# Fp32 attention and expert kernel on one core: where the tiles of the on-chip buffer begin

## The chip, the cores and the metric

The kernel runs on one core of a Trainium2 chip. The time is device microseconds of one execution on that core, and lower is better. The core has a matrix engine (PE, whose weight loads the profile lists apart as PEld), a vector engine (DVE), a scalar engine (ACT), a general engine (POOL) and a queue engine (SP) that issues most DMAs. All tiles named below lie in the on-chip buffer, 128 partitions deep; a "place" is the byte at which a tile begins within every partition. Results of matmuls go to another memory of eight banks of 2 KB, which the change doesn't touch.

## The reference

```python
# attention: 2 batches, 8 heads, 768 positions, head size 64; 4 sink positions and a window of 128
scores = scale * np.matmul(q, k.transpose(0, 1, 3, 2))
scores = np.where(is_sink | in_window, scores, -1000000000.0)
a = softmax(scores)
x = (a @ v) laid out as (1536, 512)
# eight experts, 512 -> 1024 -> 512, gate P normalised 8 times by rows and by columns
P = np.exp(logits - logits.max())
for e in range(8):
    out += P[:, e:e + 1] * (np.maximum(x @ w1[e], 0.0) @ w2[e])
# one more layer, 512 -> 2048 -> 512
h = out @ w_in
return (np.maximum(h, 0.0) ** 2) @ w_out
```

## The kernel before

**Split numbers.** Every large matrix is kept as two float tiles, a high part (name ending in h) and a low part (ending in l), and each product is three matmuls: high by high, high by low, low by high. They accumulate into one bank of 512 columns.

**Layers.** The two hidden layers are cut into 20 chunks of 512 hidden units (16 for the experts, 4 for the last layer), and the 1536 tokens into three blocks of 512; chunk 0 alone is worked in blocks of 384 tokens, beside the attention. A step "1" (`mm1`, matmuls at line 451) makes 128 hidden units by one block of tokens: 12 matmuls, in which the 128 by 128 weight piece from a `w0` tile is held in the array and 512 columns of `xh` or `xl` stream through it. A step "2" (`mm2`, line 499) makes 128 tokens by 512 outputs: 12 matmuls, in which a 128 by 128 piece of the hidden tile (`hh` or `hl`) is held and the 512 columns of a `w1` tile stream. Four steps "1" and four steps "2" alternate, 48 matmuls each. In the names of the profile `mm<-xh,w_1l` the streamed operand stands first and the held one second; the digit is the parity of the chunk.

```python
nc.tensor.matmul(
    out=ps[:, 0:n], lhsT=w[:, kc, f * 128 : (f + 1) * 128],   # mm1: held
    rhs=x[:, kc, t0 : t0 + n], ...)                            # mm1: streamed
nc.tensor.matmul(
    out=ps, lhsT=x[:, f, s], rhs=w[:, f, :], ...)              # mm2: held, streamed
```

**Around them.** `mm1_evac` (ACT line 463, DVE line 464) turns a finished bank into `hh` and `hl`; `mm2_evac` (DVE line 517) adds a finished bank to `acc`. Weights come by DMA into `wraw` and are split by ACT (line 389) and POOL (line 390). The gate (line 546) streams `xl` and `xh` through the held tile `wgz`; `x2` (line 527) transposes `acc` into `xh` and `xl` for the last layer. The attention (lines 219 to 357) takes the first 190 us or so and has matmuls of steps "1" and "2" of chunk 0 woven in.

**Order.** The order of instructions on each engine is the order in which the code is written (`manual_schedule`), and nothing in it depends on where a tile lies.

**Places.** Tiles get their places in the order in which pools are opened, each pool behind the one before, rounded to 32 bytes. `run` opens `const`, then `big` (`xh`, `xl`, `acc`, 24,576 bytes each), then `gp` (the gate's small tiles: `P`, `l2`, `mx`, `nm`, `nmb`, `rs`, `cs`, 1,344 bytes in all), then the pools of the weights, the hidden tiles and the rest. In the built program this gives:

| tiles | begin at | past a multiple of 2,048 |
|---|---|---|
| `xh`, `xl`, `acc` | 17,056; 41,632; 66,208 | 672 |
| all `w0`, `w1`, `hh`, `hl`, `wraw`, `wgz` tiles | 92,128 and on, in steps of 8,192 (`wgz` 225,248) | 2,016 |
| `pth`, `ptl` of the attention | 197,472 and on, in steps of 6,144 | 864 |

One row of a `w` or `hh` tile (512 floats) is 2,048 bytes, one row of `xh` 6,144, and a block of 512 tokens 2,048: so a streamed row begins 672 bytes past a multiple in every step "1" of 512 columns, and 2,016 past in every step "2". The held pieces of 512 bytes begin at 2,016, 480, 992 or 1,504 past, in both.

Of the kernel before, what the change touches and what calls it, by code (L numbers as in the profile page):

```python
# [9 lines left out]
F32 = mybir.dt.float32  # L10
# [23 lines left out]
NJ = (3, 4)  # L34
QKW = (QW + KW[0], QW + KW[1])
BIG = 1e30


class Kernel:
# [62 lines left out]
    def masks(self):  # L102
# [9 lines left out]
        )  # L112
        big = dict(scalar1=BIG, scalar2=-BIG, op0=ALU.mult, op1=ALU.add)
        nc.vector.tensor_tensor(out=self.m0, in0=band[:, 128:256], in1=sk[:, 0:128], op=ALU.max)
# [539 lines left out]
    def run(self):  # L654
        nc, tc = self.nc, self.tc
        ctx = self.ctx
        self.const = self.pool(ctx, "const")
        big = self.pool(ctx, "big")
        self.gp = self.pool(ctx, "gp")
        PS = bass.MemoryType.PSUM  # L660
        self.ps_mm = self.pool(ctx, "ps_mm", 2, PS)
        self.ps_sc = self.pool(ctx, "ps_sc", 2, PS)
        self.ps_pt = self.pool(ctx, "ps_pt", 2, PS)
        self.ps_xs = self.pool(ctx, "ps_xs", 2, PS)
        self.xh = big.tile([128, KD, NT], F32R, name="xh")
        self.xl = big.tile([128, KD, NT], F32R, name="xl")
        self.acc = big.tile([128, NTILE, DM], F32, name="acc")
        self.P = self.gp.tile([128, NTILE, E], F32, name="P")
        with ExitStack() as all_:
            self.reset()  # L670
            self.wp = [self.pool(all_, "wp0"), None]
            self.hp = [self.pool(all_, "hp0"), None]
            self.wraw = [self.pool(all_, "wraw0")]
            with tc.manual_schedule():
                gen = self.moe_groups(1)
                with ExitStack() as actx:
                    self.att = self.pool(actx, "att")
                    self.attraw = self.pool(actx, "attraw")
                    self.attv = self.pool(actx, "attv")
                    self.att2 = self.pool(actx, "att2", 2)  # L680
                    self.attp = self.pool(actx, "attp", 2)
                    self.att_load_qk(0)
                    self.masks_begin()
                    self.att3 = self.pool(actx, "att3", 3)
                    fill = self.phase_a(gen)
                self.phase_b(all_, 1, fill, gen)
        with tc.If(nc.values_load(self.flag, min_val=0, max_val=1)):
            with ExitStack() as all_:
                self.reset()
                with tc.manual_schedule():  # L690
                    with ExitStack() as actx:
                        self.tmp = self.pool(actx, "gtmp")
                        self.att = self.pool(actx, "gatt")
                        self.att2 = self.pool(actx, "gatt2", 2)
                        self.general_attention()
                    self.wp = [self.pool(all_, "gwp0"), None]
                    self.hp = [self.pool(all_, "ghp0"), None]
                    self.wraw = [self.pool(all_, "gwraw0")]
                    gen = self.moe_groups(0)
                    self.phase_b(all_, 0, None, gen)  # L700
# [346 lines left out]
```

## Time and profile before

| | us |
|---|---|
| median of three runs (1501.34, 1504.84, 1506.44) | 1504.84 |
| the profiled execution | 1502.89 |
| its span, first to last instruction | 1501.0 |
| busy in that span: PE | 1469.7 |
| DVE | 680.4 |
| ACT | 376.3 |
| POOL | 278.8 |

Matmuls are pipelined: one begins before the one ahead of it has drained, so the rows of the profile overlap, and a matmul's duration in a row is longer than the step from its start to the next start. What a matmul costs on a full PE is the step between two starts, or the length of a piece of the chain of waits divided by its matmuls.

### The profile page before, as it was taken

Reading aid. Unit: us, or ns where it says so; the run is one execution under the profiler, and the core shown is the slowest. Engines: PE = TensorE matmul, PEld = TensorE weight load, DVE = VectorE, ACT = ScalarE, POOL = GpSimd, SP = SyncE. Lnnn points to the kernel's source line nnn. Section 1 sums busy time; section 2 is a strip of 40 time slices with the busy share of each in tenths; the row PEclk is TensorE's granted clock in tenths of the full one; section 3 lists DMA queues with packets and bytes.
Section 4 is the critical chain, followed back from the end, with each engine's and each line's share of the span. In section 5 each row is a group of like instructions: output and inputs, shape, how many; then the busy total and the mean of one; then the engine's idle time right before and its main releaser. Section 6 shows DMA issues by size and latency. Waiting matters only on the chain.

```text
span 1501.0 us, 16714 instructions
## 1 busy us (share of the span) xinstructions
PE 1469.7 (98%) x6791; PEld 1201.9 (80%) x6791; DVE 680.4 (45%) x1372; ACT 376.3 (25%) x807; POOL 278.8 (19%) x238
## 2 busy tenths in 40 slices
PE   5899999999999999999999999999999999999998
PEld 4788887888888888888888888888888888888886
DVE  7988836242222222222222222222223789688732
ACT  5767622211111211111121111112111133232211
POOL 4533312111111211111121111111111112011100
PEclk9899999999999999999999999999999999999999
DMA  3323111000101000000100000010000122011001
GB/s 115 110 59 93 43 76 57 28 29 28 37 22 54 28 28 29 28 28 28 57 29 28 29 28 28 28 57 28 28 29 29 56 85 84 28 57 57 29 22 66
DMA packets 15045, 67.76 MB, mean 45 GB/s; under 512 B 2160, under 2 KB 4208, under 8 KB 8816
## 3 DMA queue, kind: packets, MB, share of 16 engines
q1 hardware_dynamic: 14672, 66.61, 13.3%
q8 instruction: 55, 0.90, 0.2%
q14 instruction: 30, 0.25, 0.1%
q10 hardware_dynamic: 288, 0.00, 0.0%
HBM read 63.46 MB, written 3.15 MB: 44 GB/s over the span
## 4 chain that ended last, share of the span: by engine, by line
PE 93%; DVE 5%; ACT 1%; DMA 0%; issue 0%; ACTq 0%; DVEq 0%
PE mm L451 43%; PE mm L499 43%; PE xp L347 3%; PE sc L219 1%; PE ptp L272 1%; DVE p L259 1%; DVE p L232 1%; DMA wn_i<-window 0%; DVE st L249 0%; PE mm L546 0%; DVE ptl L308 0%; DVE hl L464 0%; PE mm L527 0%; DVE rs L582 0%; ACT qkh L174 0%; ACT p L242 0%
## 5 line engine op out<-in xcount | busy, mean ns | idle before, releaser
L463 ACT ACTIVATE hh<-mm 128x512 fp32r<-128x512 f32 (+1 forms) x196 | 115.3, 588 | 810.3 <-PE mm L451 810.3
L464 DVE SCALAR_TENSOR_TENSOR hl<-mm,hh 128x512 fp32r<-128x512 f32 (+1 forms) x196 | 133.3, 680 | 387.4 <-ACT hh L463 387.4
L517 DVE SCALAR_TENSOR_TENSOR acc<-mm,P,acc 128x512 f32<-128x512 f32 x168 | 125.9, 750 | 279.8 <-PE mm L499 279.8
L451 PE MATMUL mm<-xl,w_0h 128*128 128x512 f32 (+1 forms) x496 | 193.3, 390 | 0.0
L451 PE MATMUL mm<-xh,w_0h 128*128 128x512 f32 (+1 forms) x496 | 193.0, 389 | 0.0
L451 PE MATMUL mm<-xh,w_0l 128*128 128x512 f32 (+1 forms) x496 | 191.9, 387 | 0.0
L451 PE MATMUL mm<-xh,w_1l 128*128 128x512 f32 x480 | 189.7, 395 | 0.0
L451 PE MATMUL mm<-xh,w_1h 128*128 128x512 f32 x480 | 189.3, 394 | 0.0
L451 PE MATMUL mm<-xl,w_1h 128*128 128x512 f32 x480 | 189.3, 394 | 0.0
L499 PE MATMUL mm<-w_0h,hh 128*128 128x512 f32 x480 | 188.1, 392 | 0.0
L499 PE MATMUL mm<-w_0l,hh 128*128 128x512 f32 x480 | 188.0, 392 | 0.0
L499 PE MATMUL mm<-w_1h,hl 128*128 128x512 f32 x480 | 187.4, 390 | 0.0
L499 PE MATMUL mm<-w_1h,hh 128*128 128x512 f32 x480 | 187.2, 390 | 0.0
L499 PE MATMUL mm<-w_0h,hl 128*128 128x512 f32 x480 | 187.1, 390 | 0.0
L499 PE MATMUL mm<-w_1l,hh 128*128 128x512 f32 x480 | 187.0, 389 | 0.0
L390 POOL TENSOR_TENSOR w_1l<-wraw,w_1h 128x512 fp32r<-128x512 f32 x64 | 82.1, 1292 | 434.4 <-ACT w_1h L389 434.4
L390 POOL TENSOR_TENSOR w_0l<-wraw,w_0h 128x512 fp32r<-128x512 f32 x64 | 81.9, 1289 | 368.0 <-ACT w_0h L389 368.0
L451 PEld LDWEIGHTS mm<-xl,w_0h 128*128 128x128 f32 x496 | 92.9, 187 | 21.4 <-issue 1.3
L451 PEld LDWEIGHTS mm<-xh,w_0h 128*128 128x128 f32 x496 | 92.9, 187 | 21.2 <-issue 1.1
L451 PEld LDWEIGHTS mm<-xh,w_0l 128*128 128x128 f32 x496 | 92.9, 187 | 19.9
L451 PEld LDWEIGHTS mm<-xh,w_1h 128*128 128x128 f32 x480 | 89.9, 187 | 22.1
L451 PEld LDWEIGHTS mm<-xl,w_1h 128*128 128x128 f32 x480 | 89.9, 187 | 21.7
(143 smaller groups left out, 1918.1 us busy)
## 6 DMA issues: line engine op xcount, KB each, us to landing
wraw<-w SPq DMA_DIRECT2D x32, 1024.0 KB, 4.9
wraw<-win SPq DMA_DIRECT2D x8, 1024.0 KB, 5.2
wraw<-wout SPq DMA_DIRECT2D x8, 1024.0 KB, 5.1
raw<-qkv SPq DMA_DIRECT2D x8, 624.0 KB, 4.0
raw<-qkv SPq DMA_DIRECT2D x8, 464.0 KB, 3.5
out<-acc SPq DMA_DIRECT2D x12, 256.0 KB, 2.0
vraw<-qkv SPq DMA_DIRECT2D x8, 256.0 KB, 2.7
vraw<-qkv SPq DMA_DIRECT2D x8, 192.0 KB, 2.4
```

The source lines that it names most:

```text
L219: nc.tensor.matmul(out=ps[:, 0:wd], lhsT=x[r, l * 128 : (l + 1) * 128], rhs=y[r, QW + off : QW + off + wd], start=(m == 0), stop=(m == 2),)
L232: self.nc.vector.tensor_tensor_reduce(out=p[:, a, 0:wd], in0=self.sc[u][a][:, 0:wd], in1=mask[a], scale=-(D ** -0.5), scalar=3e38, op0=ALU ...
L259: self.nc.vector.tensor_scalar(out=p[:, a, 0:wd], in0=p[:, a, 0:wd], scalar1=st[:, 2 + a : 3 + a], scalar2=None, op0=ALU.mult,)
L272: nc.tensor.transpose(ps[:, a, j * 128 : (j + 1) * 128], p[:, a, tt[a] + j * 128 : tt[a] + (j + 1) * 128], self.ident,)
L347: nc.tensor.matmul(out=o, lhsT=l, rhs=r, start=(k == 0), stop=(k == last), skip_group_check=True)
L390: nc.gpsimd.tensor_tensor(out=lo[:, s], in0=src, in1=hi.bitcast(F32)[:, s], op=ALU.subtract)
L451: nc.tensor.matmul(out=ps[:, 0:n], lhsT=w[:, kc, f * 128 : (f + 1) * 128], rhs=x[:, kc, t0 : t0 + n], start=(k == 0), stop=(k == 3 * KD - 1),)
L463: nc.scalar.activation(out=hh[:, f, 0:n], in_=ps[:, 0:n], func=AF.Relu)
L464: nc.vector.scalar_tensor_tensor(out=hl[:, f, 0:n], in0=ps[:, 0:n], scalar=0.0, in1=h32[:, f, 0:n], op0=ALU.max, op1=ALU.subtract,)
L499: nc.tensor.matmul(out=ps, lhsT=x[:, f, s], rhs=w[:, f, :], start=(k == 0), stop=(k == 3 * KD - 1),)
L517: nc.vector.scalar_tensor_tensor(out=a, in0=ps, scalar=self.P[:, ti, e : e + 1], in1=a, op0=ALU.mult, op1=ALU.add)
```

## The change

The pool `gp` is opened before `big` instead of behind it, and a pool of one tile of 8 floats (32 bytes) is opened between the two, written once by DVE.

```diff
+PAD = 8
...
         self.const = self.pool(ctx, "const")
+        self.gp = self.pool(ctx, "gp")
+        pad = self.pool(ctx, "pad")
         big = self.pool(ctx, "big")
-        self.gp = self.pool(ctx, "gp")
...
+        nc.vector.memset(pad.tile([128, PAD], F32, name="pad"), 0.0)
         self.xh = big.tile([128, KD, NT], F32R, name="xh")
```

In the built program `xh`, `xl` and `acc` then begin at 18,432, 43,008 and 67,584, that is 1,376 bytes further on and 0 past a multiple of 2,048. Everything behind `acc` moves by 32 bytes: all `w0`, `w1`, `hh`, `hl`, `wraw` and `wgz` tiles begin 0 past a multiple; the attention's tiles move by the same 32 bytes (`pth` 896 past). `ident` stays, and `P` moves to 17,056.

No instruction changes its place on any engine, nor any wait; DVE has one more. The first rows of DVE's order before (line, operation, out and in):

```order
L1043 UNCONDITIONAL_BRANCH
L76 MEMSET warm 128x1
L81 CAST acc<-acc 128x256
L82 CAST acc<-acc 128x256
L62 CAST ns_f<-ns_i 128x1
```

The same place in the changed kernel, where line numbers are one or more higher:

```order
L1047 UNCONDITIONAL_BRANCH
L668 MEMSET pad 128x8
L77 MEMSET warm 128x1
L82 CAST acc<-acc 128x256
L83 CAST acc<-acc 128x256
L63 CAST ns_f<-ns_i 128x1
```

One small write stands ahead of the one that the scalar engine's first table load goes with; nothing else has moved.

## Rows read from the trace of the kernel before

**Rows 1.** The page: span, engines' busy time, granted clock by slices, chain shares.
```profile
span 1501.0 us, 16714 instructions
PE 1469.7 (98%) x6791; PEld 1201.9 (80%) x6791; DVE 680.4 (45%) x1372; ACT 376.3 (25%) x807; POOL 278.8 (19%) x238
...
PEclk9899999999999999999999999999999999999999
...
PE 93%; DVE 5%; ACT 1%; DMA 0%; issue 0%; ACTq 0%; DVEq 0%
```

**Rows 2.** Engines' busy time in stretches: PE, PEld, DVE, ACT, POOL, clock, DMA.
```profile
400.00:800.00 400.00, 400.00 (x1739) 325.69 (x1738) 104.58 (x145) 68.00 (x121) 61.34 (x48) 1.00 0.09 32
```

**Rows 3.** The chain that ended last, in time: start us, us, what.
```profile
1.17 7.05 DMA wn_i<-window
...
263.93 11.23 PE mm L451 x48
275.16 10.90 PE mm L499 x48
286.06 11.20 PE mm L451 x48
297.26 10.90 PE mm L499 x48
...
1192.16 11.20 PE mm L451 x48
1203.36 1.75 PE mm L527 x16
...
1462.68 11.20 PE mm L451 x48
1473.88 21.80 PE mm L499 x96
```

**Rows 4.** Groups by shape: line, engine, names, shapes, count | busy us, mean ns.
```profile
L451 PE MATMUL mm<-xh,w_1l 128*128 128x512 f32 x480 | 189.7, 395 | 0.0
...
L499 PE MATMUL mm<-w_1l,hh 128*128 128x512 f32 x480 | 187.0, 389 | 0.0
L451 PE MATMUL mm<-xh,w_0l 128*128 128x512 f32 x432 | 170.4, 394 | 0.0
...
L451 PE MATMUL mm<-xh,w_0l 128*128 128x384 f32 x64 | 21.6, 337 | 0.0
```

**Rows 5.** Timeline of PE at the border of two blocks: start us, us, what.
```profile
804.93 0.39 PE L451 MATMUL mm<-xl,w_1h 128*128 128x512 f32 x1
805.17 0.39 PE L451 MATMUL mm<-xh,w_1h 128*128 128x512 f32 x1
805.40 0.39 PE L499 MATMUL mm<-w_1h,hl 128*128 128x512 f32 x1
...
806.55 0.39 PE L499 MATMUL mm<-w_1l,hh 128*128 128x512 f32 x1
806.78 0.39 PE L499 MATMUL mm<-w_1h,hl 128*128 128x512 f32 x1
```

**Rows 6.** Timeline of PE: 384-column matmuls at two places, and the gate's.
```profile
126.50 0.34 PE L451 MATMUL mm<-xh,w_0h 128*128 128x384 f32 x1
...
127.36 0.34 PE L451 MATMUL mm<-xl,w_0h 128*128 128x384 f32 x1
...
205.44 0.40 PE L546 MATMUL mm<-xh,wgz 128*128 128x512 f32 x1
...
206.84 0.40 PE L546 MATMUL mm<-xh,wgz 128*128 128x512 f32 x1
207.07 0.34 PE L451 MATMUL mm<-xl,w_0h 128*128 128x384 f32 x1
...
208.81 0.34 PE L451 MATMUL mm<-xh,w_0h 128*128 128x384 f32 x1
...
212.08 0.34 PE L451 MATMUL mm<-xh,w_0h 128*128 128x384 f32 x1
...
213.85 0.34 PE L451 MATMUL mm<-xh,w_0l 128*128 128x384 f32 x1
```

**Rows 7.** Groups by shape, weight loads of both lines.
```profile
L451 PEld LDWEIGHTS mm<-xh,w_0l 128*128 128x128 f32 x496 | 92.9, 187 | 19.9
L499 PEld LDWEIGHTS mm<-w_0l,hh 128*128 128x128 f32 x480 | 90.1, 188 | 19.3 <-issue 0.7
```

**Rows 8.** Timeline of all engines at the start.
```profile
0.80 0.06 DVE L76 MEMSET warm<- 128x1 f32 x1 [0.80 <-PEq L1033]
...
1.21 0.40 DVE L81 CAST acc<-acc 128x256 f32<-128x256 int32 x1 [0.34 <-POOL acc L79]
...
1.67 1.28 ACT L77 ACT_TABLE_LOAD   x1 [1.67 <-PEq L1033]
...
2.96 0.20 ACT L77 ACTIVATE warm<-warm 128x1 f32<-128x1 f32 x1
5.73 1.07 ACT L174 ACTIVATE qkh<-raw 128x640 fp32r<-128x640 f32 x2 [2.56 <-DMA raw<-qkv]
```

**Rows 9.** Groups by shape: transposes of the attention and of `x2`, and the gate.
```profile
L272 PE MATMUL ptp<-ident,p 128*128 128x128 f32 x176 | 32.9, 307 | 8.3 <-DVE p L259 8.3
...
L527 PE MATMUL mm<-ident,acc 128*128 128x128 f32 x48 | 5.7, 273 | 0.0
...
L546 PE MATMUL mm<-xl,wgz 128*128 128x512 f32 x12 | 4.9, 412 | 0.0
```

## The prediction

> **What bounds the kernel now.** I read the page first. PE is busy for 1469.7 of 1501.0 us, the chain that ended last is 93% PE, and the granted clock is full in nearly every slice [rows 1]. DVE, ACT and POOL have 45% and less, so an operation of theirs counts only where PE waits for it. From 264 us to the end PE never waits: the chain of waits is one row of blocks of 48 matmuls [rows 3], and a stretch of 400 us in the middle has 400.00 us of PE at clock 1.00, the 2.4 GHz level [rows 2]. What can move the time is therefore the step from one matmul's start to the next, not a wait.
>
> The chain gives that step for the two kinds of block. A block of line 451 takes 11.20 us, 233.3 ns a matmul; a block of line 499 takes 10.90 us, 227.1 ns [rows 3]. Both stream 512 columns, hold 128 by 128 weights, write the same banks and load weights in the same time, 187 and 188 ns [rows 4, 7]. What differs is where the operands lie. In both the held piece begins 480, 992, 1,504 or 2,016 bytes past a multiple of 2,048. The streamed row begins 2,016 past in line 499, so that the two distances differ by a multiple of 512; in line 451 it begins 672 past, 192 past such a multiple. The gate has other weights, but streams the same `xh` and `xl` rows: 6 steps in 1.40 us, 233.3 ns, the step of line 451 [rows 6]. So the longer step goes with the streamed tile.
>
> What is streaming and what is on top? A 384-column matmul of line 451 has steps of 173.3 ns (9 steps in 1.56 us from 207.25) [rows 6]. Against 227.1 for 512 columns that is 53.8 ns for 128 columns, 0.42 ns a column, which is one column per clock at 2.4 GHz. 512 columns then stream in 213.3 ns, and 13.8 ns in line 499 and 20.0 ns in line 451 are lost beside the streaming. Over the whole program that is the only thing that an address can give back.
>
> Two rows warn against a simple rule. The 384-column rows of the second token block begin 160 bytes past and end before the next multiple of 2,048; those of the fourth begin 1,184 past and cross it. Their steps are 172 ns (5 in 0.86 us) and 173.3 [rows 6], so crossing such a multiple costs 1 ns or so, if anything. And the same 384-column matmuls, at the same streamed places, run at 177.0 ns four microseconds later (10 steps in 1.77 us from 212.08) [rows 6]: the loss has levels into which a stream settles. At the border of two blocks line 499 begins with 230 ns (5 steps in 1.15 us) before it settles at 227 [rows 5]. I read this as weight reads and streamed reads of the same engine meeting in the buffer, with a loss that depends on how the two sequences stand to each other; no row shows the meeting itself.
>
> **The change part by part.**
>
> *The blocks of line 451.* All streamed and held rows will begin at multiples of 512, the streamed ones at multiples of 2,048. Their distance to each other becomes a multiple of 512, which line 499 has had all along. If this distance sets the level, line 451 takes the step of line 499: 11.20 - 10.90 = 0.30 us less a block. There are three groups of 480 and three of 432 [rows 4], 2,736 matmuls, 57 blocks: 57 x 0.30 = 17.1 us. All of it lies on the path, since nothing waits there [rows 2, 3]. The row bounds it from both sides: nothing, if the level isn't set by the place, and 20.0 ns x 2,736 = 54.7 us, if the loss goes altogether. I take 17.1, because line 499 is the nearest row: same shape, same engine state, with the distance that the change makes.
>
> *The blocks of line 499.* Six groups of 480 [rows 4], 2,880 matmuls, 60 blocks. Streamed and held tiles move by the same 32 bytes, so their distance stays, and I take 0. The bounds: 0.30 us a block more, if their level is an accident of their present place (18.0 us), or 13.8 ns x 2,880 = 39.7 us less, if an aligned start takes all loss away.
>
> *384-column matmuls and the gate.* Three groups of 64, 192 of the one [rows 4]; 3.7 ns between their two levels, at most 0.7 us either way; I take 0, as both levels show up at one place. Two groups of 12, 24 of the other [rows 9], x 6.2 ns = 0.15 us less.
>
> *The attention.* Its tiles all move by 32 bytes, so the distance between what it streams and holds stays; only `ident` stays where it is under the transposes of `p`. These are not bound by columns: the `x2` transposes take 1.75 / 16 = 109 ns for 128 columns, 53 ns worth of streaming [rows 3]. If each of the 176 and 48 of them [rows 9] moved by the 6.2 ns between the two levels above, that would be 1.4 us, either way. I take 0.
>
> *What is added.* One write of 32 bytes on DVE, by the nearest row 0.06 us (`warm`, one column) [rows 8]. Behind it DVE idles 0.34 us for POOL's first `acc`, and ACT begins its table load at 1.67, long after `warm` was written, and then waits 2.56 us for the first `raw` [rows 8]. The chain begins with a DMA of 7.05 us that isn't behind it [rows 3]. Cost 0; without that cover 0.06 us. DMAs, their sizes and the order on SP's queue stay.
>
> *DVE, ACT and POOL* may read or write aligned tiles faster or slower; with 45% and less [rows 1] and no PE wait behind them from 264 us on, I take 0.
>
> **The sum** is made against the profiled execution, 1502.89 us, of which 1501.0 is span and 1.9 lies around it: 17.1 + 0.15 = 17.3 us less, 1485.6. The median of the three runs, 1504.84, is 1.95 above that execution, so the forecast for a median is 1504.84 - 17.3 = 1487.6.
>
> **The rivals.**
>
> *No change.* The 20.0 and 13.8 ns may belong to the two loops rather than to places. For: no distance within line 451 shows, since all its held pieces and token blocks have one step [rows 3], and the 384-column rows have both levels at one place [rows 6]. Against: I find nothing else that sets the two lines apart. The time is the median, 1504.8. The Trainium skill speaks for this rival: its page "TensorE: Matmul & The Clock Gate", section "Step-by-step: what each phase is for", says that PE reads streamed and held operands through two ports and that loading the next weights takes nothing from the running matmul; section "Wait — 56ns, not 53.3ns?" gives 215.7 ns for 512 columns of bf16 at the full clock. By that rule no place matters. The trace disagrees with the figure, with 227.1 and 233.3 ns [rows 3], though for 4-byte data; whether it disagrees with the rule is what the change will show.
>
> *More than that.* What counts is where a row begins, and an aligned start loses less than any row of before shows, in both lines. If half of the loss of line 499 goes, both come to 220.2 ns: 60 x 0.33 + 57 x 0.63 = 55.7 us, a time of 1449; if all goes, 54.7 + 39.7 = 94.4 us, 1410. For: no row of before has an aligned start on a full PE. Against: the 672, 160 and 1,184 bytes of the 384-column rows made 1 ns of difference.
>
> *Slower.* The blocks of line 499 are fast because of their present place and drop to the longer level once moved, while those of line 451 stay there. Every block then takes 11.20: 60 x 0.30 = 18.0 us, 1522.8. It decides as soon as a block of line 499 takes over 11.05 us while line 451 gains nothing. For: line 499 needs some 5 matmuls to settle [rows 5], so its level is not given by the shape alone. Against: its two operands keep their distance.
>
> That the change doesn't do what it says is hardly open: the places are fixed when the program is built. The attention's tiles don't become aligned, and I count nothing for them.
>
> **How the numbers follow.** Line 451 takes the step of line 499: 0.48, own range 1483 to 1493 (the 384-column and transpose terms and the spread of the runs). No change: 0.22. More: 0.15. Slower: 0.15. A measurement of this kernel can tell about 0.3%, 4.5 us, from no change. So faster 0.48 + 0.15 = 0.63, same 0.22, slower 0.15. The range runs from 1476 to 1526: it holds the first two cases and most of the slower one, and leaves out nearly all of the larger gain and the worst of the loss, less than 2 in 10.
>
> **What would show it.** In the chain of waits of the changed kernel, blocks of line 451 at 10.90 us and of line 499 still at 10.90 show the first case; 11.20 and 10.90 unchanged, the second; both under 10.8, the third; line 499 at 11.2, the fourth. The gate's steps must go the way of line 451. It would be wrong in its reason, though not in sign, if line 451 gained and line 499 moved as well, since the distance within line 499 does not change.

## The result and the profile after

The changed kernel takes 1483.17 us in the median of four runs (1482.14 to 1484.84), the kernel before 1503.38 in four (1501.34 to 1506.44): a ratio of 0.9865, with an interval of 0.9843 to 0.9886, 20 us or 1.3% faster. Ratios here and below are against the kernel before on the same chip. The profiled execution takes 1482.95 us, of which 1481.1 is span, against 1502.89 and 1501.0.

The page's busy times and its shares of the chain; each line answers to one of [rows 1]:

```profile
span 1481.1 us, 16715 instructions
...
PE 1448.7 (98%) x6791; PEld 1201.6 (81%) x6791; DVE 679.6 (46%) x1373; ACT 376.2 (25%) x807; POOL 278.5 (19%) x238
...
PE 93%; DVE 5%; ACT 1%; DMA 0%; issue 0%; ACTq 0%; DVEq 0%
```

PE is the only engine whose busy time moved by more than 1 us: 1469.7 to 1448.7, with as many instructions, and as before 98% of the span. A share alone would show nothing here. DVE, ACT and POOL take the time that they took.

The stretch from 400 to 800 us (PE, PEld, DVE, ACT, POOL, clock, DMA), as in [rows 2]:

```profile
400.00:800.00 400.00, 400.00 (x1766) 331.24 (x1765) 106.36 (x148) 70.24 (x124) 63.72 (x50) 1.00 0.10 32
```

PE is full in both kernels and at the same granted clock of 1.00, but 1,766 matmuls fit where 1,739 did: 226.5 ns each against 230.0.

The chain that ended last (start us, us, what), as in [rows 3]. Line numbers are one higher than before, so line 452 is the former 451 and line 500 the former 499:

```profile
262.96 10.92 PE mm L452 x48
273.88 10.88 PE mm L500 x48
284.76 10.88 PE mm L452 x48
295.64 10.88 PE mm L500 x48
...
1454.23 21.77 PE mm L500 x96
```

Both kinds of block now take 10.88 us, where they took 11.20 and 10.90. Counted over the chain from the first full block on, line 451 had 2,640 matmuls of 233.3 ns, and line 452 has as many of 226.7: 17.6 us. Line 499 had 2,688 of 227.1, and line 500 has as many of 226.7: 1.1 us. Together 18.7 of the 19.9 us between the two spans. Nearly all the rest lies ahead of the first full block, which begins 0.97 us earlier (263.93 and 262.96). Some 0.5 us of that is seen in steps: by the starts in the trace, 88 full steps of line 451 with 512 columns fall there from 233.2 to 227.9 ns, while those of line 499 stay at 229. The remainder isn't put down to the change: in six further runs below the block begins anywhere from 264.2 to 266.4, and the same changed kernel, run once more, has it at 264.2. From the first full block to the end, before takes 1237.07 us and after 1218.14.

The timeline of PE at a border of the same kind as in [rows 5], from streams of `xh` and `xl` to those of a `w1` tile (start us, us, what):

```profile
795.73 0.39 PE L452 MATMUL mm<-xh,w_1h 128*128 128x512 f32 x1
795.96 0.39 PE L500 MATMUL mm<-w_1h,hl 128*128 128x512 f32 x1
...
797.32 0.39 PE L500 MATMUL mm<-w_1h,hl 128*128 128x512 f32 x1
```

Six steps in 1.36 us, 226.7 ns, from the first one of a block on. Before, line 499 began each block with some five steps of 230 ns. Now the stream changes its tiles without a change of its rhythm, here and at the borders the other way (six steps in 1.36 us from 785.08 on).

### The profile page after: what moved, and what is told of

Same layout as the page of the kernel before. It is cut to its first block, busy times and chain, and to the rows that moved or that the text cites. A ratio compares the mean times of both kernels' runs of the same rounds, so it can differ in the third digit from the quotient of the medians.

```text
span 1481.1 us, 16715 instructions
## 1 busy us (share of the span) xinstructions
PE 1448.7 (98%) x6791; PEld 1201.6 (81%) x6791; DVE 679.6 (46%) x1373; ACT 376.2 (25%) x807; POOL 278.5 (19%) x238
## 4 chain that ended last, share of the span: by engine, by line
PE 93%; DVE 5%; ACT 1%; DMA 0%; issue 0%; ACTq 0%; DVEq 0%
PE mm L500 44%; PE mm L452 43%; PE xp L348 3%; PE sc L220 1%; DVE p L260 1%; PE ptp L273 1%; DVE p L233 1%; DVE st L250 1%; DMA wn_i<-window 0%; ACT qkh L175 0%; DVE ptl L309 0%; PE mm L547 0%; DVE hl L465 0%; ACT p L243 0%; PE mm L528 0%; DVE rs L583 0%
## 5 line engine op out<-in xcount | busy, mean ns | idle before, releaser
L500 PEld LDWEIGHTS mm<-w_0h,hh 128*128 128x128 f32 x480 | 90.1, 188 | 19.3 <-issue 0.7
L500 PEld LDWEIGHTS mm<-w_0l,hh 128*128 128x128 f32 x480 | 90.1, 188 | 19.2 <-issue 0.7
```

The costliest lines, as they stand in the source:

```text
L500: nc.tensor.matmul(out=ps, lhsT=x[:, f, s], rhs=w[:, f, :], start=(k == 0), stop=(k == 3 * KD - 1),)
```

## Which part of the change does it

The change does three things at once: it moves `big` against the weights, it makes every large tile of the two lines begin at a multiple of 2,048 bytes, and it makes all of them aligned by any smaller power of two. The theory was that only the distance between what is streamed and what is held counts. The first three kernels ran together on one chip.

**Only the pools exchanged.** `gp` lies ahead of `big`, without the pad. All large tiles of the two lines then begin 2,016 bytes past a multiple of 2,048, and the distance from streamed to held rows is a multiple of 512.

```diff
         self.const = self.pool(ctx, "const")
+        self.gp = self.pool(ctx, "gp")
         big = self.pool(ctx, "big")
-        self.gp = self.pool(ctx, "gp")
```

> The gate's small pool lies in front of the large ones, and no pad: every large tile begins 2,016 bytes past a multiple of 2,048, where the weight and hidden tiles lay before, and only xh, xl and acc have moved (from 672 past). No tile begins at a multiple of 64. Theory of the distance (streamed and held row 0 apart modulo 512): blocks of line 451 at 10.90 us or less, of line 499 at 10.88 to 10.90, 1483 to 1487 us. Rival of the alignment (rows that begin at multiples of 64 or of 2,048 stream faster): line 451 stays at 11.20, 1503 us.

Measured: 1485.81 us (1485.28 to 1488.24), a ratio of 0.9888 (0.9864 to 0.9911). Its chain:

```profile
700.71 10.88 PE mm L451 x48
711.59 10.88 PE mm L499 x48
```

The same 10.88 us as after the whole change, with no tile of these matmuls at a multiple of even 64 bytes.

**Only the pad.** 32 bytes ahead of `big`, with `gp` left behind it. The held tiles then begin at multiples of 2,048 and `xh` at 704 past one, so the distance within line 452 is what it was before.

```diff
+        pad = self.pool(ctx, "pad")
         big = self.pool(ctx, "big")
         self.gp = self.pool(ctx, "gp")
...
+        nc.vector.memset(pad.tile([128, PAD], F32, name="pad"), 0.0)
```

> The pad of 32 bytes in front of the large tiles and the pools in their old order: the weight and hidden tiles begin at multiples of 2,048, xh, xl and acc 704 past one, so every row begins at a multiple of 64, and the distance between streamed and held in line 451 is that of before (192 modulo 512). Theory of the distance: line 451 at 11.20 us a block, line 499 at 10.90, 1503 us. Rival of the alignment to 64: both at 10.88, 1483 us; of the alignment to 2,048: only line 499 gains, its blocks at 10.88 in place of 10.90, 1502 us.

Measured: 1505.27 us (1502.91 to 1507.33), a ratio of 1.001 (0.9997 to 1.0022).

```profile
641.45 11.20 PE mm L452 x48
652.65 10.90 PE mm L500 x48
```

The blocks of before, to the last digit. Line 500 now streams and holds rows at multiples of 512 and gains nothing by that. The beginnings alone do nothing; the exchange does it all.

**Places one by one.** A kernel of matmuls alone: two tiles `x` and `w` that begin at multiples of 2,048, a warm-up of 96 matmuls, then 36 settings of 48 matmuls each. A setting shifts the streamed row or the held piece by so many bytes, or takes fewer columns.

```diff
+            r = k % 4
+            a = ox // 4 + 512 * r
+            b = ow // 4 + 512 * ((k // 4) % 4) + 128 * r
+            return dict(
+                out=ps[:, 0:n], lhsT=w[:, b : b + 128], rhs=x[:, a : a + n],
...
```

> Nothing but matmuls on PE, 36 settings of 48 matmuls each, one line a setting: a streamed row of 512 columns (or 256, 384, 448) and a held piece of 128 by 128, with the byte places of the two rows set one by one. The output isn't the reference's; all the rest is left out. Theory of the distance: 226.7 ns a matmul at equal places modulo 512 whatever the places are (0, 32, 64, 2016 past), more at a distance of 192 or 64, and some period of the step in the distance. Rival of the alignment: the step goes with the streamed row's own place alone, 226.7 at 0 and longer at 32 and 2016, whatever the held row does. With less to collide the loss beside the streaming should not grow with the columns: 173.3 ns at 384 columns if it is a constant 13.3, 170 if it goes with the columns.

It took 430.17 us. The chain gives one row for each setting (start us, us, line):

```profile
35.84 10.88 PE mm L50 x48
46.72 11.20 PE mm L53 x48
57.93 11.00 PE mm L56 x48
...
80.14 11.20 PE mm L62 x48
...
124.96 10.88 PE mm L74 x48
...
213.47 11.38 PE mm L98 x48
...
335.79 10.92 PE mm L131 x48
346.72 11.20 PE mm L134 x48
357.92 8.35 PE mm L137 x48
366.26 5.75 PE mm L140 x48
```

In this order: both at 0; the streamed row 32, 64, 128, 256 and 4 bytes on; both 2,016 on; streamed 672 and held 2,016 on, the places of the kernel before; then 384 and 256 columns with both at 0. A block's time has the settling in it, so here is the step over the second half of each setting, from the starts in the trace, for 512 columns:

| streamed / held, bytes on | ns | clocks beyond 512 |
|---|---|---|
| 0 / 0 | 226.7 | 32 |
| 256, 512 or 1,024 / 0; 0 / 256 | 226.7 | 32 |
| 32 / 32; 64 / 64; 2,016 / 2,016 | 226.7 | 32 |
| 672 / 2,016 | 233.3 | 48 |
| 64 / 0; 320 / 0 | 228.8; 228.9 | 37 |
| 32, 96, 128, 160, 192, 224 / 0 | 233.3 to 234.1 | 48 to 50 |
| 0 / 32; 64; 128 | 233.4; 233.4; 232.3 | 48; 48; 46 |
| 4 / 0; 0 / 4 | 236.8; 232.4 | 56; 46 |

Three things follow. The two steps of the real kernel come out of two tiles and nothing else. The distance decides whether more than 226.7 ns is taken, and where both begin doesn't: 32, 64 and 2,016 on together cost nothing. And the distance counts modulo 256 bytes, where 512 had been assumed: 64 and 320 bytes give 228.8 and 228.9 ns, 192 and 448 give 233.4 and 233.3. How much is lost isn't given by it alone: 128 and 384 give 233.5 and 232.3. The same stretch also clears the other engines (columns as above):

```profile
35.84:417.00 381.16, 381.16 (x1727) 316.33 (x1726) 0.00 (x0) 0.00 (x0) 0.00 (x0) 1.00 0.00 1
```

DVE, ACT and POOL do nothing in it and DMA has a share of 0.00, with the same steps. So it isn't other engines' use of the buffer that costs line 451 its 6.7 ns.

## Back in the real kernel: 128 and 256 bytes apart

From the sweep two kernels follow that differ only in a second pad, behind `acc` and ahead of the weights. With 128 bytes all large tiles are still aligned to 128, but line 452 streams and holds 128 apart modulo 256; with 256 bytes it is back to equal places modulo 256, though not modulo 512. The cut shows the pad of 128 bytes; the other has 64 floats in place of 32.

```diff
         big = self.pool(ctx, "big")
+        pad2 = self.pool(ctx, "pad2")
...
         self.acc = big.tile([128, NTILE, DM], F32, name="acc")
+        nc.vector.memset(pad2.tile([128, 32], F32, name="pad2"), 0.0)
```

> The changed kernel with one more pad, of 128 bytes between acc and the weight tiles: xh, xl and acc begin at multiples of 2,048, the weight and hidden tiles 128 past. Every row is still aligned to 128 bytes; only the distance in line 452 (451 before) changes, from 0 to 128, and in line 500 it stays 0. Theory of the distance: line 452 back at about 232.3 ns a matmul, the step of this distance in the sweep, 11.15 us a block, line 500 at 10.88 to 10.90; 57 blocks x 0.27 = 15 us more than the changed kernel, 1498 us. Rival of the alignment to 64 or 128: nothing is lost, 1483 us.

Measured: 1503.62 us (1501.22 to 1506.57), a ratio of 0.9997 (0.9985 to 1.001).

```profile
708.20 11.19 PE mm L452 x48
719.40 10.89 PE mm L500 x48
```

The expectation had 11.15 us a block and 1498, from the 232.3 ns of the sweep's 0 / 128, and missed by 5.6 us. The block took 11.19, 233.1 ns a step. By the starts in the trace its steps alternate between some 229 and 237 ns, as those of the sweep's 128 / 0 do and those of 0 / 128 don't.

> The same with a pad of 256 bytes: the weight and hidden tiles begin 256 past a multiple of 2,048 and no longer at multiples of 512. Theory of the distance with the period of 256 bytes that the sweep shows: line 452 at 10.88 us as in the changed kernel, 1483 us. Were the period 512, as the prediction had it, or 2,048, as the change has it: line 452 at 11.15 to 11.20, 1498 to 1501 us.

Measured: 1485.79 us (1484.36 to 1486.45), a ratio of 0.9881 (0.9861 to 0.9901).

```profile
700.75 10.88 PE mm L452 x48
711.63 10.88 PE mm L500 x48
```

128 bytes take the whole gain away and 256 leave it. The distance modulo 256 bytes between streamed and held rows is thus shown as the cause in the kernel itself, both ways; by what mechanism it costs time is the next question.

## Why the distance costs something: a reading that fell

The prediction read the loss as the engine's weight reads meeting its streamed reads. If so, fewer held columns, read for a shorter time, should lose less. A second sweep holds 96, 64 and 32 columns at equal places and at 64 and 128 bytes apart, and tries distances and column counts that the first left out.

```diff
-                out=ps[:, 0:n], lhsT=w[:, b : b + 128], rhs=x[:, a : a + n],
+                out=ps[0:m, 0:n], lhsT=w[:, b : b + m], rhs=x[:, a : a + n],
```

> Matmuls alone again, the rest left out, 41 settings of 48: more distances (in steps of 16 bytes and some odd ones), held pieces of 96, 64 and 32 columns in place of 128, and streamed rows of 128 to 480 columns. If the loss beside the streaming comes from the reads of the next held piece, it shrinks with that piece at distance 0: about 32 clocks for 128 columns, 24 for 96, 16 for 64, 8 for 32. If it is a fixed cost of going from one matmul to the next, it stays near 32 for all of them. If some distance lost less than 32 clocks at 512 columns, it would make a kernel faster than the changed one; from the period seen I expect none below 226.7 ns.

It took 454.91 us. Chain rows: the streamed row 88 bytes on; then equal places with 128, 96, 64 and 32 held columns.

```profile
169.08 11.48 PE mm L86 x48
...
236.49 10.88 PE mm L104 x48
247.38 11.04 PE mm L107 x48
...
280.73 11.04 PE mm L116 x48
...
313.74 11.10 PE mm L125 x48
```

Groups by shape, the weight loads of the same four (line, engine, names, shapes, count, then busy us, mean ns and idle us):

```profile
L104 PEld LDWEIGHTS mm<-x,w 128*128 128x128 f32 x48 | 9.0, 188 | 1.9
...
L107 PEld LDWEIGHTS mm<-x,w 128*96 128x96 f32 x48 | 7.7, 161 | 3.3
...
L116 PEld LDWEIGHTS mm<-x,w 128*64 128x64 f32 x48 | 6.4, 134 | 4.6
...
L125 PEld LDWEIGHTS mm<-x,w 128*32 128x32 f32 x48 | 5.2, 109 | 5.8
```

The load falls from 188 to 109 ns and the settled step rises, from 226.7 to 230.0, 229.7 and 231.6. A loss by the number of weight reads would have fallen to a quarter. The reading falls in this form. Fewer held columns do lose less at 128 bytes apart (231.6, 229.4 and 230.1 ns for 96, 64 and 32, against 233.5 for 128 in the first sweep), and at 64 apart there is no order (233.2, 228.2 and 231.8, against 228.8). So a part of the load in the loss isn't excluded; a loss in proportion to its reads at equal places is. The distances that this sweep adds at 128 held columns, between 12 and 252 bytes, give 230 to 240 ns, the highest at 88. At 252 it is 230.0, where the first sweep's 0 / 4, the same modulo 256, had 232.4. At 128 and 192 columns the step is 111.7 ns, the same for both, and so isn't set by columns at all.

A third sweep lets places alternate from one matmul to the next, to see whether a streamed row must agree with its own held piece or with the one that is loaded meanwhile; it also tries column counts between 416 and 512, and 124, 120 and 112 held columns.

```diff
-a = ox // 4 + 512 * r
-b = ow // 4 + 512 * ((k // 4) % 4) + 128 * r
+a = ox[k % 2] // 4 + 512 * r
+b = ow[k % 2] // 4 + 512 * ((k // 4) % 4) + 128 * r
```

> Matmuls alone, the rest left out, 34 settings of 48. The theory that held and streamed reads meet in the buffer has lost its simplest form (32 held columns lost no less than 128). What is left of it: the loss depends on the distance between the row that streams and the held piece that is loaded meanwhile, which is that of the next matmul. Places alternate here between 0 and d, d being 32, 64, 128 or 192. If it is the next held piece: 226.7 ns where the next held piece is level with the streamed row, though its own is d off, and 229 to 233.5 where the own is level and the next one d off. If it is the matmul's own held piece: the other way round. If only the streamed rows' distance to each other counts: both alike. Streamed rows of 416 to 508 columns at distance 0: a fixed loss of 32 clocks gives n + 32 throughout; a start that waits for a raster gives steps that jump with n, as 448 and 480 columns (38 and 40 clocks lost) hint.

It took 413.79 us. Chain rows: all equal; own piece equal and the next one 64 off; own 64 off and the next equal; 0 and 256 alternating; 472 columns; 120 held columns.

```profile
36.11 10.88 PE mm L50 x48
...
91.41 11.11 PE mm L65 x48
102.53 11.11 PE mm L68 x48
...
235.22 10.88 PE mm L104 x48
...
289.19 10.24 PE mm L119 x48
...
368.13 11.20 PE mm L143 x48
```

Inconclusive on the mechanism. With 64 bytes, both ways of pairing give 231.7 ns; with 128 bytes an equal own piece gives 228.4 and an equal next one 230.0, with 32 and 192 bytes 231.8 and 231.7 against 233.7 and 233.3. Neither piece alone brings the step down to 226.7, only both do, with one exception (streamed alternating by 192 bytes over a held 0: 226.7). At equal places 472 columns lose 40 clocks and 416 lose 32, and 120 held columns lose 48. Of the 111 settings of the three sweeps 62 settle within 0.6 clocks of 32, 40 or 48 beyond their columns, which looks like two sequences that lock into a rhythm. What these are stays open.

## Does the pad bring anything?

The change and the exchange alone once more, side by side on one chip.

> The changed kernel as it is, beside the one with the pools swapped and no pad, on one chip. If the distance alone matters, the pad brings nothing: both within 0.15% of each other, at about 0.987 of the time before, with blocks of 48 at 10.88 us in both lines.

> The pools swapped, no pad. Theory of the distance: the same time as the changed kernel within 0.15% (2 us). If starts at multiples of 64 or 2,048 bring something of their own, outside the blocks of 48 (attention, splitting), this one is slower by 2 us or more, as the first runs of the two (1483.2 and 1485.8 us, on their own chips) would have it.

Measured: with the pad 1484.12 us (1481.96 to 1485.95), a ratio of 0.9869 (0.9851 to 0.9887); without it 1484.98 (1482.64 to 1487.73), 0.9873 (0.9854 to 0.9892). The chains, with the pad and then without:

```profile
275.15 10.88 PE mm L500 x48
286.03 10.88 PE mm L452 x48
```

```profile
275.98 10.88 PE mm L499 x48
286.86 10.88 PE mm L451 x48
```

From the first full block to the end the two take 1217.97 and 1218.04 us. The pad and the multiples of 2 KB bring nothing that can be measured.

## Why the prediction was right, point by point

**What bounds the kernel.** Right. No wait appeared or went, the clock stayed at 1.00, and all the time that can be put down to the change is in the step of a matmul.

**The blocks of line 451.** The forecast was that they take the step of line 499, because their distance becomes that of line 499: 17.1 us. Measured are 0.32 us a block, 17.6 us for the 55 blocks from the first full one on, and 0.5 us for the steps ahead of it: 18.1. The cause is confirmed both ways, by the exchange alone and by 128 bytes between. Mis-sized is the step taken: 227.1 ns is line 499's mean with its settling, and the settled step is 226.7.

**The blocks of line 499.** Taken as 0, measured 56 x 0.02 = 1.1 us less from the first full block on. The prediction said that it would be wrong in its reason if line 499 moved as well, since its distance doesn't change. The move is real but small and has a visible cause, in the rows that the prediction used itself: five steps of 230 ns at each border are 5 x 3.3 = 17 ns, 0.02 us a block, and they are gone since both kinds of block keep one rhythm. An aligned start isn't what did it: with the pad alone line 500 is aligned and stays at 10.90, with the exchange alone line 499 isn't and takes 10.88. The term left out was the influence of one block on the start of the next. Neither bound was touched.

**Gate and 384 columns.** The gate has three groups of eight. By the starts in the trace the first now steps at 226.6 ns, where it had 233.1; the other two, each behind transposes of line 556, step at 231.9, between 224 and 236, where they had 233.3. So only one group went the whole way of line 452, worth 0.07 us together where 0.15 was taken. The 384-column rows still show both levels: nine steps in 1.56 us, 173.3 ns, and others up to 185. Their mean rose from 174.4 to 175.9 (139 steps under 190 ns), 0.2 us more in all: zero was right to that.

**Attention and the write added.** Nothing can be seen of either; the first full block's start varies by 3.5 us among these runs.

**The sum.** 17.3 was forecast, and the terms that can be named measured 18.1 + 1.1 + 0.1 - 0.2 = 19.1, against 19.9 between the spans; the rest is within the spread of the first block's start. The forecast for the median, 1487.6, lies 4.4 us above the measured 1483.17: 2.9 by the size of the gain (20.2 between the medians), and 1.5 because the median before was 1504.84 in three runs and is 1503.38 in four. The measured median is only 0.2 us inside the first case's own range, 1483 to 1493; that it fell inside is luck.

**The rivals.** "No change" falls with the exchange and the 128 bytes, and so does the thought that the two loops themselves set the two steps: the bare sweep makes both steps with one loop. The rule behind it, in the Trainium skill, page "TensorE: Matmul & The Clock Gate", section "Step-by-step: what each phase is for", is that loading the next weights takes nothing from the running matmul. No run here settles it: at equal places a load of 109 ns costs no less than one of 188, while at 128 bytes apart narrower held pieces lose less. What the prediction drew from it, that no place matters, is refuted by 226.7 against 233.3 ns. "More" falls: in the 111 settings of the three sweeps none of 512 columns and 128 held goes below 226.7. "Slower" falls: line 500 doesn't leave its level in any of the kernels, since its tiles keep their distance wherever they are moved together.

**Right for a partly wrong reason.** The prediction let the distance count modulo 512, and it is 256; that changed no number here, since 0 modulo 512 is 0 modulo 256 too. Its picture of weight reads meeting streamed reads didn't hold in the form that could be tested. The estimate needed neither, only that two loops of one shape differ in nothing but a distance, and that one of them already had the distance that the other was to get.

## What to carry to other kernels

Where matmuls fill an engine, look at the step between two starts for each loop apart; a difference between loops of the same shape is a loss that no share of busy time, no wait and no clock showed here. Then print where the streamed and the held rows begin and make them agree modulo 256 bytes: here small tiles of 1,344 bytes (5 x 256 + 64) between two large pools cost 1.3% of the kernel, and moving them away, or a distance brought up to a multiple of 256, gave it back. That was seen for 512 columns and 128 held ones. For other counts measure first, since the best place isn't the same: 480 columns settle at 216.6 ns with equal places and at 213.3 with 128 bytes between, and 64 held columns at 229.7 with equal places and at 228.2 with 64 bytes between.

## What the runs showed of the hardware

- A 512-column matmul of these 4-byte tiles with 128 held columns steps at 226.7 ns at best, 32 clocks of 2.4 GHz beyond its columns, and at 228.8 to 240 ns at every constant distance tried that is no multiple of 256 bytes, the lowest at 64 and the highest at 88.
- The period of the distance is 256 bytes: 256, 512 and 1,024 bytes cost nothing, 128 costs as much as 32 (233.5 and 233.3 ns).
- At equal places the loss doesn't shrink with fewer held columns: with a load of 109 ns in place of 188 the step is 231.6 ns, longer than with the full width. At 128 bytes apart it does, from 233.5 ns with 128 held columns to 229.4 with 64.
- It often comes in levels: 32, 40 or 48 clocks in 62 of 111 settings, also for other column counts (384 at 173.3 ns is 32 beyond, 472 is 40). Why is open.
- No other engine takes part: the steps are the same with DVE, ACT, POOL and DMA at rest.
